# Seven products in place of eight: y times v_in by Strassen's scheme, with the combined weights kept in DRAM

## The chip, the cores and the metric

The kernel runs on one core of a Trainium2 chip. The metric is the device time of one execution in microseconds. All inputs lie in DRAM at the start, the output lies there at the end, and nothing is computed on the host except the layout of the inputs.

## The reference

Attention over 4 batches, 8 heads, 576 positions and 64 channels, with a causal window of 128 and a linear bias; then two gated layers over the 2304 tokens. Only the last lines matter for the change:

```python
attn_out = _attn_ref(q, k, v)                  # (4, 8, 576, 64)
x = attn_out.transpose(0, 2, 1, 3).reshape(2304, 512)
a = x @ w1; b = x @ w2                         # 512 -> 1024
y = ((a * b) @ w3) @ w_out                     # 1024 -> 1024 -> 512
h = y @ v_in                                   # 512 -> 2048   (moe2_w_in)
g = h * np.clip(h + 3.0, 0.0, 6.0) / 6.0
return (g @ v_out).astype(np.float32)          # 2048 -> 512   (moe2_w_out)
```

The weights arrive as 64-bit floats and are unpacked to 32-bit ones on the chip.

## The kernel before

Matrix products run in a 32-bit format that TensorE rounds. To keep the accuracy, each operand is split into a rounded part `hi` and the rest `lo` (`split`, L74: ACT copies, VectorE or GpSimd subtracts), and each product is three matmuls, hi x hi, hi x lo and lo x hi (`mm3`, L46 to L49). Each loads a 128x128 tile of one operand and streams the columns of the other.

The first half runs over batches: attention, then for each half batch of 288 tokens eight `ab_unit`s (a, b and their product) and four `y_unit`s (L504), which write y transposed to DRAM (`yT`). The matrices w3 and w_out are multiplied beforehand. During the last batch, at the units listed in `AT`, the weights of the second half are loaded (1 MB for each of 16 groups `f` of 128 of the 2048 columns of v_in, together with the matching rows of v_out), unpacked (`unpack`, L55) and split (`v2_split`, L523), and y of the first block is loaded and split too (`y_load`, `y_split`). The other groups follow during the second half's first block.

The second half runs over blocks of 512 tokens (four, and a last one of 256), and in each over the 16 groups. `h_unit` (L607) multiplies y by one group of v_in: four chunks of 128 channels, twelve matmuls into one bank, for which four banks of PSUM stand ready (two of `ps_mm`, two of `ps_h`). ACT applies the relu of h + 3 (L620), DVE takes the minimum with 6 times h (L621, the gate), and the result is split. `o_unit` (L627) multiplies it by v_out, 128 tokens at a time, into four banks that collect over all groups; it follows two units behind (`LAG`). All split weights stay in SBUF, 16 groups in hi and lo.

The order of the instructions on each engine is fixed when the program is built: the framework simulates a timeline and lists, for each engine, the ready instruction of the highest priority, so that the order can differ from that of the source. Instructions wrapped in `in_order(True, ...)` (L51) keep the order of the source among themselves. On the chip each engine then follows its list. Tiles with one tag share buffers, and a new tile waits until the old one is no longer read; a pool that is opened after others have been closed takes their room and waits for their last readers in the same way.

```python
units = [(j, f) for j in range(len(blocks)) for f in range(KG)]
LAG = 2
for idx, (j, f) in enumerate(units):
    h_unit(j, f)
    if idx >= LAG:
        o_unit(*units[idx - LAG])
```

Of the kernel before, what the change touches and what calls it, by code (L numbers as in the profile page):

```python
# [8 lines left out]
F32 = mybir.dt.float32  # L9
# [8 lines left out]
P = 128  # L18
# [4 lines left out]
def tile_attention_moe_moe2(ctx: ExitStack, tc: tile.TileContext, qT, kT, vm, vt, wo, w3, w12, w2x, out):  # L23
# [59 lines left out]
    yT = dpool.tile([KD, P, NT], F32, name="yT")  # L83
# [432 lines left out]
    TB = 512
    NPRE = 3
    v2 = {}

    def v2_load(f, tmp):  # L520
        load(("v2", f), w2x[f], tmp)

    def v2_split(f, pool, lo_eng):  # L523
        old = NPRE <= f < NPRE + KF
        hi, lo = (
            (blk if old else pool).tile(
                [P, 2 * KD, P], F32R, name=f"v2{t[0]}{f}", **({"tag": f"{t}{f - NPRE}"} if old else {})
            ) for t in ("hi", "lo")
        )
        split(flat(hi), flat(lo), unpack(rawt.pop(("v2", f)), pinned=True), lo_eng)  # L530
        v2[f] = (hi, lo)

    blocks = [(t, min(TB, NT - t)) for t in range(0, NT, TB)]
    yb = {}

    yraw = {}

    p2 = [("v", f) for f in range(KG)]
    p2.insert(NPRE, ("y", 0))

    def p2_load(i):
        if i < len(p2):
            (v2_load if p2[i][0] == "v" else y_load)(p2[i][1], dec)

    def p2_make(i, pool):
        if i < len(p2):
            if p2[i][0] == "v":
                v2_split(p2[i][1], pool, nc.vector)
            else:
                y_split(0, pool)  # L550
            p2_load(i + 2)

    def y_load(j, tmp):
        t0, n = blocks[j]
        t = tmp.tile([P, KD, TB], F32, tag="raw", name=f"yraw{j}")
        nc.sync.dma_start(out=t[:, :, 0:n], in_=yT[:, :, t0 : t0 + n].rearrange("c p t -> p c t"))
        yraw[j] = t

    def y_split(j, pool):
        t0, n = blocks[j]  # L560
        yh = pool.tile([P, KD, TB], F32R, tag="yh2", bufs=1, name=f"yh2_{j}")
        yl = pool.tile([P, KD, TB], F32R, tag="yl2", bufs=1, name=f"yl2_{j}")
        t = yraw.pop(j)
        for i in range(2):
            c = slice(2 * i, 2 * i + 2)
            nc.scalar.copy(yh[:, c, 0:n], t[:, c, 0:n])  # L566
            nc.gpsimd.tensor_tensor(out=yl[:, c, 0:n], in0=t[:, c, 0:n], in1=f32(yh[:, c, 0:n]), op=ALU.subtract)  # L567
        yb[j] = (yh, yl)
# [6 lines left out]
    for b in range(B):  # L575
        if b == B - 1:
            apool_ctx.close()
            ps_h = ctx.enter_context(tc.tile_pool(name="ps_h", bufs=2, space=PSUM))
            ps_o = ctx.enter_context(tc.tile_pool(name="ps_o", bufs=1, space=PSUM))

            AT = [3, 6, 9, 11, 13, 15, 17, 19, 21]
            dec = ctx.enter_context(tc.tile_pool(name="dec", bufs=2, side="right"))
            pre = ctx.enter_context(tc.tile_pool(name="pre", bufs=1, side="right"))
            p2_load(0)
            p2_load(1)
        for iu, u in enumerate(units):
# [12 lines left out]
    p1.close()  # L599


    vpool = ctx.enter_context(tc.tile_pool(name="vpool", bufs=1))
    r2 = ctx.enter_context(tc.tile_pool(name="r2", bufs=2))
    g2p = ctx.enter_context(tc.tile_pool(name="g2p", bufs=3))
    g2 = {}

    def h_unit(j, f):  # L607
        t0, n = blocks[j]
        yh, yl = yb[j]
        hi, lo = v2[f]  # L610
        if f % 2 == 0:
            ps = ps_mm.tile([P, 512], F32, tag="mm", name=f"h_{j}_{f}")
        else:
            ps = ps_h.tile([P, TB], F32, tag="h", name=f"h_{j}_{f}")
        for c in range(KD):
            mm3(ps[:, 0:n], hi[:, c, :], lo[:, c, :], yh[:, c, 0:n], yl[:, c, 0:n], c == 0, c == KD - 1)
        rl = r2.tile([P, TB], F32, tag="rl", name=f"rl_{j}_{f}")
        gh = g2p.tile([P, TB], F32R, tag="g2h", name=f"g2h_{j}_{f}")
        gl = g2p.tile([P, TB], F32R, tag="g2l", name=f"g2l_{j}_{f}")
        nc.scalar.activation(rl[:, 0:n], ps[:, 0:n], AF.Relu, bias=three[:, 0:1], scale=1.0)  # L620
        nc.vector.scalar_tensor_tensor(out=rl[:, 0:n], in0=rl[:, 0:n], scalar=6.0, in1=ps[:, 0:n], op0=ALU.min, op1=ALU.mult)  # L621
        split(gh[:, 0:n], gl[:, 0:n], rl[:, 0:n], nc.vector)
        g2[j, f] = (gh, gl)
# [21 lines left out]
    units = [(j, f) for j in range(len(blocks)) for f in range(KG)]
    LAG = 2
    for idx, (j, f) in enumerate(units):
        h_unit(j, f)
        if idx >= LAG:
            o_unit(*units[idx - LAG])  # L650
        if j == 0:
            p2_make(f + len(AT), vpool)
        if j + 1 < len(blocks):
            if f == KG - 3:
                y_load(j + 1, dec)
            if f == KG - 1:
                y_split(j + 1, pre if j % 2 else vpool)
    for u in units[-LAG:]:
        o_unit(*u)
# [61 lines left out]
```

## Time and profile before

| | |
|---|---|
| timed runs, median of 3 | 904.21 us (903.53 to 905.42) |
| profiled execution, span | 907.7 us, 3.5 us over that median |
| TensorE (PE) busy | 888.4 us, 98% |
| VectorE (DVE) busy | 435.3 us, 48% |
| ScalarE (ACT) busy | 402.0 us, 44% |
| GpSimd (POOL) busy | 143.4 us, 16% |
| DMA | 74.0 MB, mean 82 GB/s |
| mean granted clock of TensorE | 0.993 of 2.4 GHz |

The span is that of the profiled execution alone, from its first to its last instruction; all rows below are from it. Busy time of PE is time in which some matmul is under way; matmuls overlap, so a sum of durations says more than the time they cost, and the distance from the start of one to the start of the next is what one costs in a dense stream. PEld is the loading of the stationary operand, which runs beside the matmuls. In the rows, "a<-b" means that a is written from b; "[0.84 <-DVE rl L621]" behind an instruction is how long its engine stood idle before it, and what it waited for. SPq is the queue of the engine that issues most of the DMAs.

### The profile page before, as it was taken

The numbers are of one execution on the slowest core, as the hardware profiler recorded it, in microseconds if no ns is written. First come the engines' busy times: TensorE is split into PE (matmuls) and PEld (weight loads), VectorE is DVE, ScalarE is ACT, GpSimd is POOL, SyncE is SP. The second block draws the span as 40 slices with busy tenths as digits, with TensorE's granted clock in tenths as the row PEclk, the third lists the DMA queues.
The fourth block names the chain that finished last, engine by engine and source line by source line (L and its number), as shares of the span: only waits on it lengthen the run. The fifth ranks groups of instructions, "written<-read, shape, count | busy, mean of one in ns | idle before, by whom it ended". The sixth has DMA issues, their size and how long they took to land.

```text
span 907.7 us, 13401 instructions
## 1 busy us (share of the span) xinstructions
PE 888.4 (98%) x5216; PEld 780.2 (86%) x5216; DVE 435.3 (48%) x935; ACT 402.0 (44%) x856; POOL 143.4 (16%) x226
## 2 busy tenths in 40 slices
PE   6999899999999999999999999999999999999998
PEld 5645689999999999999999888888888888888897
DVE  6788565665766736451436587232223222322232
ACT  7566455665665645552334565322232222222232
POOL 5500302333331322220020002010010001000000
PEclk9999799999999999999999999999999999999999
DMA  9977312323332212103142455120001000100000
GB/s 272 287 294 262 92 60 66 93 66 85 72 79 60 63 52 66 40 2 119 47 166 93 165 186 189 43 70 1 1 1 46 1 1 1 47 1 1 17 30 24
DMA packets 23151, 74.00 MB, mean 82 GB/s; under 512 B 2864, under 2 KB 8496, under 8 KB 18480
## 3 DMA queue, kind: packets, MB, share of 16 engines
q1 hardware_dynamic: 23088, 73.15, 26.0%
q8 instruction: 41, 0.67, 0.3%
q14 instruction: 22, 0.18, 0.1%
HBM read 63.70 MB, written 9.44 MB: 81 GB/s over the span
## 4 chain that ended last, share of the span: by engine, by line
PE 88%; DMA 1%; ACT 0%; DVE 0%; POOL 0%; issue 0%; ACTq 0%
PE ab L47 8%; PE ab L48 8%; PE ab L49 8%; PE o L47 7%; PE o L49 7%; PE o L48 7%; PE h L47 7%; PE h L49 7%; PE h L48 7%; PE X L290 4%; PE y L47 4%; PE y L49 4%; PE y L48 3%; PE pt L261 2%; PE s L203 2%; PE s L206 1%
## 5 line engine op out<-in xcount | busy, mean ns | idle before, releaser
L47 PE MATMUL ab<-xh,w12h 128*128 128x288 f32 x512 | 155.6, 304 | 0.1
L48 PE MATMUL ab<-xl,w12h 128*128 128x288 f32 x512 | 152.0, 297 | 0.0
L49 PE MATMUL ab<-xh,w12l 128*128 128x288 f32 x512 | 151.6, 296 | 0.0
L621 DVE SCALAR_TENSOR_TENSOR rl<-rl,h 128x512 f32<-128x512 f32 (+1 forms) x80 | 50.7, 634 | 200.7 <-ACT rl L620 200.7
L620 ACT ACTIVATE rl<-h,three 128x512 f32<-128x512 f32 (+1 forms) x80 | 51.7, 647 | 200.5 <-PE h L49 196.5
L47 PE MATMUL h<-yh,v2h 128*128 128x512 f32 (+1 forms) x320 | 118.5, 370 | 0.8 <-DVE rl L621 0.8
L49 PE MATMUL h<-yh,v2l 128*128 128x512 f32 (+1 forms) x320 | 118.2, 369 | 0.0
L48 PE MATMUL h<-yl,v2h 128*128 128x512 f32 (+1 forms) x320 | 117.9, 368 | 0.0
L47 PE MATMUL o<-v2h,g2h 128*128 128x512 f32 x288 | 112.9, 392 | 0.0
L48 PE MATMUL o<-v2l,g2h 128*128 128x512 f32 x288 | 112.3, 390 | 0.0
L49 PE MATMUL o<-v2h,g2l 128*128 128x512 f32 x288 | 111.6, 391 | 0.0
L47 PEld LDWEIGHTS ab<-xh,w12h 128*128 128x128 f32 x512 | 96.5, 189 | 1.2 <-ACT asb L497 0.5
L48 PEld LDWEIGHTS ab<-xl,w12h 128*128 128x128 f32 x512 | 96.6, 189 | 0.5 <-issue 0.2
L49 PEld LDWEIGHTS ab<-xh,w12l 128*128 128x128 f32 x512 | 96.5, 188 | 0.0
L243 POOL TENSOR_SCALAR pr<-pr,rc 128x256 f32<-128x256 f32 (+1 forms) x128 | 61.4, 497 | 135.4 <-DVE rc L236 73.2
L76 DVE TENSOR_TENSOR g2l<-rl,g2h 128x512 fp32r<-128x512 f32 (+1 forms) x80 | 54.8, 685 | 44.6 <-ACT g2h L75 44.3
L47 PE MATMUL y<-g,Wh 128*128 128x288 f32 x256 | 75.9, 299 | 0.2 <-ACT yf L511 0.2
L567 POOL TENSOR_TENSOR yl<-yraw,yh 128x1024 fp32r<-128x1024 f32 (+1 forms) x10 | 24.0, 2423 | 327.2 <-ACT yh L566 327.2
L49 PE MATMUL y<-g,Wl 128*128 128x288 f32 x256 | 75.4, 297 | 0.0
L48 PE MATMUL y<-g,Wh 128*128 128x288 f32 x256 | 75.0, 295 | 0.0
L47 PEld LDWEIGHTS h<-yh,v2h 128*128 128x128 f32 x320 | 60.1, 188 | 12.1 <-DVE rl L621 1.3
L48 PEld LDWEIGHTS h<-yl,v2h 128*128 128x128 f32 x320 | 60.1, 188 | 11.0
(106 smaller groups left out, 1640.9 us busy)
## 6 DMA issues: line engine op xcount, KB each, us to landing
raww<-in_w_dram SPq DMA_DIRECT2D x16, 1024.0 KB, 6.6
rawv<-in_w2x_dram SPq DMA_DIRECT2D x16, 1024.0 KB, 4.9
rawq<-in_qT_dram SPq DMA_DIRECT2D x24, 288.0 KB, 4.3
rawk<-in_kT_dram SPq DMA_DIRECT2D x24, 288.0 KB, 4.6
yT<-yf SPq DMA_DIRECT2D x32, 144.0 KB, 1.8
out_dram<-ob SPq DMA_DIRECT2D x18, 256.0 KB, 2.0
rawwo<-in_wo_dram SPq DMA_DIRECT2D x4, 1024.0 KB, 8.3
yraw<-yT SPq DMA_DIRECT2D x4, 1024.0 KB, 5.2
```

Of the source, the lines that this page charges most:

```text
L47: nc.tensor.matmul(ps, lh, rh, start=first, stop=False)
L48: nc.tensor.matmul(ps, lh, rl, start=False, stop=False)
L49: nc.tensor.matmul(ps, ll, rh, start=False, stop=last)
L76: lo_eng.tensor_tensor(out=lo, in0=src, in1=f32(hi), op=ALU.subtract)
L203: in_order(n == NP + 1 and j == 0 and h == 0, nc.tensor.matmul(o, sp1["qs"][:, qc], sp1["kh"][:, kc], start=True, stop=False))
L206: nc.tensor.matmul(o, sp1["qs"][:, qc], sp1["kl"][:, kc], start=False, stop=True)
L243: nc.gpsimd.tensor_scalar(out=o, in0=o, scalar1=rc[:, 2 * j + h : 2 * j + h + 1], scalar2=1.0, op0=ALU.mult, op1=ALU.mult)
L261: nc.tensor.transpose(ps[:, o : o + P], prob[n, j][:, h, c : c + P], ident)
L290: last_pe["x", n, h] = nc.tensor.matmul(X[:, c0 : c0 + nq], l, r, start=bank not in seen, stop=last[bank] == idx, skip_group_check=True)
L567: nc.gpsimd.tensor_tensor(out=yl[:, c, 0:n], in0=t[:, c, 0:n], in1=f32(yh[:, c, 0:n]), op=ALU.subtract)
L620: nc.scalar.activation(rl[:, 0:n], ps[:, 0:n], AF.Relu, bias=three[:, 0:1], scale=1.0)
L621: nc.vector.scalar_tensor_tensor(out=rl[:, 0:n], in0=rl[:, 0:n], scalar=6.0, in1=ps[:, 0:n], op0=ALU.min, op1=ALU.mult)
```

## The change

The 2304 tokens are taken in three blocks of 768, each as two halves of 384 tokens; the 512 channels are two halves, and the 16 groups of v_in are paired, group p with group p + 8. For each block and pair, y times v_in is then a product of 2x2 blocks, made with seven products (the Winograd form of Strassen's scheme) in place of eight: sums of y's quarters (`y_sums`, GpSimd) and of v_in's quarters (`va_make`, GpSimd) are made first, and seven products (`PRODUCTS`) of two chunks each, 384 columns wide, go through the two banks of `ps_mm`. DVE adds them up to the four results (`s1`, `u2`, `u3`, c22, c21, c12); one result is added up in PSUM alone. `ps_h` is gone; the products with v_out collect in six banks. They are cut into twelve `o_jobs` per pair, which are put between the products of the next pair (`QUOTA`).

The combined weights of a pair, seven tiles in hi and lo, are 14 KB per partition, so not all fit in SBUF: each is stored in DRAM (`vad`, and `vod` for v_out) once made, and fetched again in each later block (`fetch`, two pairs ahead). Four of the eight pairs are made in the last batch of the first half, the other four in block 0, at its even positions. The pools of the second half (`ypool` first) are opened when all of the first half's are closed; `blk`, which outlived the first half before, is now among those. y of block 0 is therefore loaded after the first half's last use of that room, by ACT's queue; the loads of later blocks stand in SP's queue, in the order of the source, with the fetches and stores. The split tiles of y have one buffer each.

```diff
-    yT = dpool.tile([KD, P, NT], F32, name="yT")
+    yT = dpool.tile([2, KD // 2, P, NT], F32, name="yT")
+    NPR = KG // 2
+    vad = dpool.tile([NPR, P, 2, 7, 2 * P], F32, name="vad")
+    vod = dpool.tile([NPR, P, 2, 2, DM], F32, name="vod")
...
-    blk = ctx.enter_context(tc.tile_pool(name="blk", bufs=1))
     p1 = ExitStack()
+    blk = p1.enter_context(tc.tile_pool(name="blk", bufs=1))
...
+    PRODUCTS = [(A11, B11), (S2, T2), (A12, B21), (S3, T3), (S1, T1), (A22, T4), (S4, B22)]
+    def dma(dst, src):
+        in_order(not p1_open[0], nc.sync.dma_start(out=dst, in_=src))
...
+    def va_tile(p, right):
+        pool = vR if right else vL
+        va[p] = pool.tile([P, 2, 7, 2 * P], F32R, tag="va", bufs=2, name=f"va{p}")
+    def vo_tile(p, right):
+        vo[p] = pool.tile([P, 2, 2, DM], F32R, tag="vo", bufs=1 if right else 2, name=f"vo{p}")
+    def va_make(p, right):
+        r = unpack(rawt.pop(("v2", 2 * p)), pinned=True)
+        q = [r[:, i * 2 * P : (i + 1) * 2 * P] for i in range(4)]
+        st = sR.tile([P, 3, 2 * P], F32, tag="st", name=f"st{p}")
+        nc.gpsimd.tensor_tensor(out=st[:, 0, :], in0=q[0], in1=q[2], op=ALU.subtract)
+        nc.gpsimd.tensor_tensor(out=q[2], in0=q[2], in1=q[3], op=ALU.add)
+        nc.gpsimd.tensor_tensor(out=st[:, 1, :], in0=q[2], in1=q[0], op=ALU.subtract)
+        nc.gpsimd.tensor_tensor(out=st[:, 2, :], in0=q[1], in1=st[:, 1, :], op=ALU.subtract)
+        t = va_tile(p, right)
+        split(flat(t[:, 0, 0:4, :]), flat(t[:, 1, 0:4, :]), r, nc.vector)
+        split(flat(t[:, 0, 4:7, :]), flat(t[:, 1, 4:7, :]), flat(st), nc.vector)
+        late.append((vad[p], t))
...
+    def y_load(j):
+        for ci in range(2):
+            t = ypool.tile([P, 2, 2 * TH], F32, tag=f"yraw{ci}", name=f"yraw{j}_{ci}")
+            src = yT[ci, :, :, 2 * TH * j : 2 * TH * (j + 1)].rearrange("c p t -> p c t")
+            if j == 0:
+                nc.scalar.dma_start(out=t, in_=src)
             else:
+                dma(t, src)
+            yraw[j, ci] = t
+    def y_sums(j):
+        for ci in range(2):
+            t = yraw.pop((j, ci)).rearrange("p c (h t) -> p (c h) t", h=2)
+            tm = ypool.tile([P, 3, TH], F32, tag=f"tm{ci}", name=f"tm{j}_{ci}")
+            nc.gpsimd.tensor_tensor(out=tm[:, 0, :], in0=t[:, 3, :], in1=t[:, 1, :], op=ALU.subtract)
+            nc.gpsimd.tensor_tensor(out=t[:, 1, :], in0=t[:, 1, :], in1=t[:, 0, :], op=ALU.subtract)
+            nc.gpsimd.tensor_tensor(out=tm[:, 1, :], in0=t[:, 3, :], in1=t[:, 1, :], op=ALU.subtract)
+            nc.gpsimd.tensor_tensor(out=tm[:, 2, :], in0=tm[:, 1, :], in1=t[:, 2, :], op=ALU.subtract)
...
+    def y_splits(j):
+        for _, k in PRODUCTS:
+            hi = ypool.tile([P, 2, TH], F32R, tag=f"yh{k}", name=f"yh{j}_{k}")
+            lo = ypool.tile([P, 2, TH], F32R, tag=f"yl{k}", name=f"yl{j}_{k}")
+            for ci in range(2):
+                split(hi[:, ci, :], lo[:, ci, :], yraw.pop((j, ci, k)), nc.vector)
...
-            ps_h = ctx.enter_context(tc.tile_pool(name="ps_h", bufs=2, space=PSUM))
-            AT = [3, 6, 9, 11, 13, 15, 17, 19, 21]
+            AT = [2, 5, 8, 10, 12, 14, 16, 18]
...
+    def h_pair(j, p, between):
+        a, b_ = bank(0), None
+        product(0, a, True, True)
+        s1 = new("s1")
+        nc.scalar.copy(s1, a[:, 0:TH])
+        between(0)
+        b_ = bank(1)
+        product(1, b_, True, True)
+        u2 = new("u2")
+        nc.vector.tensor_tensor(out=u2, in0=b_[:, 0:TH], in1=s1, op=ALU.add)
+        between(1)
+        product(2, a, False, True)
+        gate(a[:, 0:TH], (0, 0))
+        between(2)
+        product(3, b_, False, True)
+        u3 = new("u3")
+        nc.vector.tensor_tensor(out=u3, in0=b_[:, 0:TH], in1=s1, op=ALU.add)
+        between(3)
+        a = bank(2)
+        product(4, a, True, True)
+        c = new("c22")
+        nc.vector.tensor_tensor(out=c, in0=a[:, 0:TH], in1=u3, op=ALU.add)
+        gate(c, (1, 1))
+        between(4)
+        b_ = bank(3)
+        product(5, b_, True, True)
+        c = new("c21")
+        nc.vector.tensor_tensor(out=c, in0=u3, in1=b_[:, 0:TH], op=ALU.subtract)
+        gate(c, (1, 0))
+        between(5)
+        product(6, a, False, True)
+        c = new("c12")
+        nc.vector.tensor_tensor(out=c, in0=a[:, 0:TH], in1=u2, op=ALU.add)
+        gate(c, (0, 1))
+        between(6)
...
+    QUOTA = [2, 2, 2, 1, 2, 2, 1]
+    y_load(0)
+    y_sums(0)
+    y_splits(0)
...
+    for n, (j, pos) in enumerate(units):
+        p = ORDER[j][pos]
+        if n == 0:
+            fetch(1)
+        fetch(n + 2)
...
+        gs = h_pair(j, p, between)
+        jobs = o_jobs(j, pos, gs, vo[p])
+        if j + 1 < NBLK:
+            if pos == NPR - 4:
+                y_load(j + 1)
+            if pos == NPR - 2:
+                y_sums(j + 1)
+            if pos == NPR - 1:
+                y_splits(j + 1)
```

`product(i, ps, first, last)` is six matmuls (`mm3` for two chunks); `gate` is relu, gate and split of one result, as in `h_unit`; `bank(n)` takes the next tile of `ps_mm`.

## Rows read from the trace of the kernel before

**Rows 1.** The page: busy time, share of the span and instructions of each engine.

```profile
span 907.7 us, 13401 instructions
...
PE 888.4 (98%) x5216; PEld 780.2 (86%) x5216; DVE 435.3 (48%) x935; ACT 402.0 (44%) x856; POOL 143.4 (16%) x226
```

**Rows 2.** Two stretches of the second half: length, busy time by engine, clock, DMA.

```profile
515.00:560.00 45.00, 44.16 (x193) 35.81 (x192) 36.34 (x44) 29.99 (x37) 0.00 (x0) 1.00 0.47 167
...
600.00:850.00 250.00, 250.00 (x1095) 205.25 (x1094) 67.53 (x97) 64.84 (x100) 8.24 (x4) 1.00 0.04 13
```

**Rows 3.** Groups by form: line, engine, tiles, count | busy, mean ns | idle before.

```profile
L620 ACT ACTIVATE rl<-h,three 128x512 f32<-128x512 f32 x64 | 44.1, 690 | 176.9 <-PE h L49 173.0 <-DMA yT<-yf 4.0
L621 DVE SCALAR_TENSOR_TENSOR rl<-rl,h 128x512 f32<-128x512 f32 x64 | 43.9, 688 | 176.8 <-ACT rl L620 176.8
L75 ACT CAST g2h<-rl 128x512 fp32r<-128x512 f32 x64 | 39.8, 622 | 40.7 <-DVE rl L621 40.6
...
L500 DVE TENSOR_TENSOR asb<-ab,asb 128x288 f32<-128x288 f32 x64 | 29.2, 456 | 62.4 <-PE ab L49 52.5 <-PE pt L261 9.2 <-ACT xf L303 0.3
...
L76 POOL TENSOR_TENSOR xl<-xf,xh 128x288 fp32r<-128x288 f32 x30 | 25.1, 853 | 49.7 <-ACT xh L75 49.7
...
L567 POOL TENSOR_TENSOR yl<-yraw,yh 128x1024 fp32r<-128x1024 f32 x8 | 21.0, 2650 | 244.6 <-ACT yh L566 244.6
...
L76 DVE TENSOR_TENSOR v2l<-rawv,v2h 128x1024 fp32r<-128x1024 f32 x16 | 20.0, 1250 | 11.6 <-ACT v2h L75 11.6
L69 DVE SCALAR_TENSOR_TENSOR rawv<-rawv 128x1024 int32<-128x1024 int32 x16 | 19.6, 1226 | 7.1 <-ACT rawv L64 6.4
...
L65 DVE TENSOR_SCALAR rawv<-rawv 128x1024 int32<-128x1024 int32 x16 | 11.0, 690 | 2.0 <-DMA rawv<-in_w2x_dram 2.0
...
L620 ACT ACTIVATE rl<-h,three 128x256 f32<-128x256 f32 x16 | 7.6, 476 | 23.6 <-PE h L49 23.5
...
L621 DVE SCALAR_TENSOR_TENSOR rl<-rl,h 128x256 f32<-128x256 f32 x16 | 6.7, 421 | 23.9 <-ACT rl L620 23.9
L75 ACT CAST g2h<-rl 128x256 fp32r<-128x256 f32 x16 | 6.5, 406 | 7.5 <-DVE rl L621 7.5
```

**Rows 4.** Timeline of one unit of 512 tokens: start, length, engine, operation.

```profile
641.73 0.39 PE L49 MATMUL h<-yh,v2l 128*128 128x512 f32 x1
...
642.21 0.69 ACT L620 ACTIVATE rl<-h,three 128x512 f32<-128x512 f32 x1 [3.38 <-PE h L49]
...
642.93 0.69 DVE L621 SCALAR_TENSOR_TENSOR rl<-rl,h 128x512 f32<-128x512 f32 x1 [3.37 <-ACT rl L620]
```

**Rows 5.** A stretch of the last y units alone (288 columns).

```profile
499.00:511.00 12.00, 12.00 (x93) 12.00 (x92) 1.20 (x3) 1.00 0.64 212
```

**Rows 6.** Timeline, last block: relu of its fourth and its fifteenth unit.

```profile
866.00 0.47 ACT L620 ACTIVATE rl<-h,three 128x256 f32<-128x256 f32 x1 [1.26 <-PE h L49]
...
896.68 0.48 ACT L620 ACTIVATE rl<-h,three 128x256 f32<-128x256 f32 x1 [1.43 <-PE h L49]
```

**Rows 7.** Instructions of h alone, during the last batch of the first half.

```profile
460.00:490.00 30.00, 6.53 (x24) 4.23 (x24) 0.00 (x0) 0.00 (x0) 1.00 0.41 144
```

**Rows 8.** Timeline where the second half starts.

```profile
516.34 1.26 ACT L620 ACTIVATE rl<-h,three 128x512 f32<-128x512 f32 x2 [3.95 <-DMA yT<-yf]
...
517.80 0.50 PE L47 MATMUL h<-yh,v2h 128*128 128x512 f32 x1 [0.84 <-DVE rl L621]
```

**Rows 9.** DMA: the weights' loads on the page; the first 50 us.

```profile
rawv<-in_w2x_dram SPq DMA_DIRECT2D x16, 1024.0 KB, 4.9
...
DMA packets 2998, 14.45 MB, mean 289 GB/s; under 512 B 431, under 2 KB 623, under 8 KB 1775
```

**Rows 10.** Timeline in block 0, POOL and DVE.

```profile
560.91 4.81 POOL L567 TENSOR_TENSOR yl<-yraw,yh 128x1024 fp32r<-128x1024 f32 x2 [91.77 <-ACT yh L566]
...
563.77 2.49 DVE L76 TENSOR_TENSOR g2l<-rl,g2h 128x512 fp32r<-128x512 f32 x1 [0.69 <-ACT g2h L75]
```

**Rows 11.** A stretch of the first half with gaps of PE.

```profile
100.00:150.00 50.00, 47.75 (x288) 40.36 (x288) 32.59 (x72) 27.72 (x61) 11.15 (x20) 0.93 0.20 57
```

More of the change, by code (lines that the diff above doesn't have):

```diff
@@ L559, in y_split @@
[L559 to L568, printed above, removed]
+        nc.sync.dma_start(out=yT[d % 2, d // 2, :, t0 : t0 + HS], in_=yf)
@@ L599, in tile_attention_moe_moe2 @@
     p1.close()
-    vpool = ctx.enter_context(tc.tile_pool(name="vpool", bufs=1))
+    p1_open[0] = False
+    ypool = ctx.enter_context(tc.tile_pool(name="ypool", bufs=1))
+    vL = ctx.enter_context(tc.tile_pool(name="vL", bufs=1))
     r2 = ctx.enter_context(tc.tile_pool(name="r2", bufs=2))
[L604 to L623, printed above, removed]
@@ L645, in tile_attention_moe_moe2 @@
[L645 to L659, printed above, removed]
+    g2p = ctx.enter_context(tc.tile_pool(name="g2p", bufs=8))
@@ new lines, in tile_attention_moe_moe2, with product, new, gate @@
+    po = {}
+    ob_ = {}
+    def h_pair(j, p, between):
+        w = va[p]
+        def product(i, ps, first, last):
+            k, y = PRODUCTS[i]
+            yh, yl = yc[j, y]
+            for c in range(2):
+                cols = slice(c * P, (c + 1) * P)
+                mm3(
+                    ps[:, 0:TH], w[:, 0, k, cols], w[:, 1, k, cols], yh[:, c, :], yl[:, c, :],
+                    first and c == 0, last and c == 1, skip_group_check=True,
+                )
+        def new(tag):
+            return r2.tile([P, TH], F32, tag=tag, bufs=2 if tag in ("rl", "u2", "u3") else 1, name=f"{tag}_{j}_{p}")
+        gs = {}
+        def gate(h, q):
+            rl = new("rl")
+            g_ = g2p.tile([P, 2, TH], F32R, tag="g2", name=f"g2_{j}_{p}_{q[0]}{q[1]}")
+            nc.scalar.activation(rl, h, AF.Relu, bias=three[:, 0:1], scale=1.0)
+            nc.vector.scalar_tensor_tensor(out=rl, in0=rl, scalar=6.0, in1=h, op0=ALU.min, op1=ALU.mult)
+            split(g_[:, 0, :], g_[:, 1, :], rl, nc.vector)
+            gs[q] = g_
+        def bank(n):
+            return ps_mm.tile([P, 512], F32, tag="mm", name=f"h_{j}_{p}_{n}")
+        a, b_ = bank(0), None
[32 more added lines that the diff above has]
+        between(6)
+        return gs
@@ new lines, in tile_attention_moe_moe2, with fetch @@
+    QUOTA = [2, 2, 2, 1, 2, 2, 1]
+    units = [(j, pos) for j in range(NBLK) for pos in range(NPR)]
+    def fetch(n):
+        if n >= len(units):
+            return
+        j, pos = units[n]
+        p = ORDER[j][pos]
+        if j == 0 and p >= NEARLY:
+            return
+        if not (j == 0 and p >= NEARLY - 2):
+            dma(f32(va_tile(p, pos % 2 == 0)), vad[p])
+        if not (j == 0 and p == NEARLY - 1):
+            dma(f32(vo_tile(p, pos % 2 == 0)), vod[p])
+    y_load(0)
+    y_sums(0)
@@ L662 @@
+    for job in jobs:
+        job()
 _OUTS = [((2304, 512), "float32")]
```

164 lines of the change are left out of this document (102 added, 62 removed).

## The prediction

> **What bounds the kernel now.** Read the busy times first: PE 888.4 us of a 907.7 us span, DVE and ACT under half [rows 1]. The stretches then show that this holds in the second half, which the change rewrites: from 600 to 850 us PE is busy for 250.00 of 250.00 us with 1095 matmuls, DVE for 67.5 us; only from 515 to 560, while weights are still being made, do DVE (36.3 of 45) and ACT come near it [rows 2]. The by-form rows price the DVE, ACT and POOL instructions [rows 3]. The timeline of one unit shows what follows an h matmul group: relu, then gate, then cast and subtract, the gate 0.03 us after the relu's end [rows 4]. So a matmul taken away is worth its spacing, and a new wait of PE costs its whole length.
>
> **The matmuls.** Spacing, not duration, is what one costs, for they overlap. 512 columns: 250.00/1095 = 0.2283 us [rows 2]. 288 columns: 12.00/93 = 0.129, say 0.130 since a matmul on an edge is counted [rows 5]. 256 columns: eleven units of the last block take 896.68 - 866.00 = 30.68 us, 2.789 each; less six out-matmuls (1.370) leaves 1.419 for twelve: 0.118 [rows 6]. There is no 384 in the trace. Between 256 and 512 it is 0.173, between 288 and 512 it is 0.172; I take 0.173. Its bounds are the pro rata values, 0.171 from 512 and 0.1775 from 256.
>
> Before, h has 64 units of 12 at 512 columns and 16 of 12 at 256: 768 x 0.2283 + 192 x 0.118 = 198.0 us. After, 3 blocks x 8 pairs x 7 products x 6 = 1008 at 0.173: 174.4 us. **Saved: 23.6 us** (19 to 25.5 by the bounds). The products with v_out are 864 of 512 columns before and after, 197 us: no change. A pair is now 42 x 0.173 + 36 x 0.2283 = 15.5 us of PE. The matmuls of h that now run early, 24 between 460 and 490 us [rows 7], are only moved, and cost nothing if the first half had no gaps that they filled; if it had, they hid up to 6.5 us. I take 1 us, since matmuls of ab and y fill the other time there.
>
> **DVE and ACT per pair.** For 384 columns halfway between the rows of 256 and 512: relu 0.583, gate 0.555, cast 0.514; the adds and the subtract I take at 0.555 too (the 288-column multiply took 0.456) [rows 3]. A pair is 5 adds, 4 gates, 4 subtracts: 13 x 0.555 = 7.2 us of DVE in 15.5; ACT's copy, 4 relus and 4 casts are under 5. Neither bounds a pair alone.
>
> **The edge of a pair.** h loses the two banks of `ps_h`: its seven products now go through two. The last one (product 6) ends in a bank that the next pair's product 0 wants. Between them stands one out-job. The add of c12 can start 0.48 us after the last matmul's start in [rows 4], at 384 columns some 0.42; with 0.555 and 0.03 it frees the bank at 1.01 us. PE has that matmul (0.173) and three of 512: 0.86 us. So it falls short by 0.15 us, 24 times: **3.6 us**. Below: nothing, if more out-jobs are put in between when the program is ordered. Above: if DVE takes gate (1,0)'s subtract first, that chain (add, relu, gate, cast, subtract and four hops) ends 3.30 us after product 5's last matmul, against 2.83 when c12 could start: 0.47 more, 0.62 per pair, 15 us.
> The trace has one wait of this kind: at 517.80, with all four banks of h full, PE waited 0.84 us until the gate had freed one [rows 8]. The Trainium skill (Perfetto Trace Analysis, Matmuls) says that independent groups should rotate through different PSUM banks, so that one is emptied while the next is computed; the change goes from four to two. If the rule is taken to mean that each pair pays such a wait, the term is 24 x 0.84 = 20 us in place of 3.6; the wait agrees with it in kind, and nothing here shows it for each pair.
>
> **Where the second half starts.** Before, y of block 0 was loaded and split during the first half. Now its room is free only after the last ab unit; four y units (96 matmuls, 12.5 us) cover. The first product needs one part of the two loads (5 us by the 1024 KB loads of [rows 9]), two casts, two subtracts: about 7 us, covered. The second needs T2, the third of four sums per half, and POOL computes them: 0.853 us at 288 columns, 2.65 at 1024, so 1.09 at 384 [rows 3]; seven of them after the load make 13 us and the split 14, against 13.5 when it is due. Then pair 0 has no out-jobs between its products, 7.3 us of PE, while DVE has 14 subtracts (7.8 us), the pair's 7.2 and v_in's combinations for pair 1: shift 0.69, unpack 1.23, subtract 1.25 and 0.94 for the extra three quarters, 4.1 us. I take **5 us**. Below: 0. Above: 19, the second rival.
> One thing there is worse than the sum of busy times: at 563.77 a subtract of 512 columns took 2.49 us in place of 0.69, while POOL was at work from 560.91 to 565.72 [rows 10]. If sums and subtracts take turns like this, the seventh sum ends 7 x 1.09 + 6 x 0.555 = 11 us after the load, T2 is split at 17 and product 1 is some 3.5 us late; my 5 us contain that. The Trainium skill (SBUF — State Buffer, Who interferes with whom) says that a DVE instruction with two SBUF inputs and a GpSimd instruction that reads SBUF contend for one port pair. By it they do take turns; without it product 1 would be 0.5 us late, and the term about 2.
>
> **Two changes of block.** y's split tiles are single now, so block j+1's splits wait for pair 7's products: 14 subtracts more in 31 us of two pairs, 22 us of DVE. That fits; the list of instructions is ordered ahead of time, and in [rows 7] it moved h forward by 40 us, so I expect them spread. 1 us each: **2 us**, from 0 to 12 (all splits behind the last product).
>
> **Block 0 makes weights.** Four pairs x 7.3 us of DVE (4.1, and 3.17 for v_out), pairs 8 x 7.2, splits 7.8: 95 of 124 us, 76%; before, 81% left PE at 44.2 of 45 [rows 2]. With two banks in place of four, a 1.2 us unpack in front of an eviction shows: **2 us**, 0 to 10.
>
> **The stream.** Each pair of blocks 1 and 2 fetches 1.84 + 1.05 = 2.89 MB in 15.5 us: 186 GB/s. The first 50 us ran at 289 GB/s [rows 9]. SP issues in order, and the fetch of a right-hand v_out tile waits for the out-jobs of the pair before it, so two pairs' transfers bunch: the next v_in tile lands some 2.89/0.289 = 10 us plus a couple after, inside 15.5. Also y (1.57 MB) fits once: 15.4, tight. Block 0 moves 11.5 MB of stores, 8.4 of raw weights and 6.8 fetched again: 215 GB/s, under 289 too. I take 0.
>
> **Sum.** 907.7 - 23.6 + 1 + 3.6 + 5 + 2 + 2 = 897.7 us in the profiled execution's terms. Its span lies 3.5 us over the timed median of 904.2, so the forecast is **894 us**.
>
> **Rivals.**
> *All covered* (0.17): the order fills every edge, start and block change cost under 5 us together: 880 to 888. For it: PE idled 0.84 us in the second half of before although DVE was at 81%. Against it: four banks then, and a second half already prepared.
> *The two-bank ring* (0.15): 0.62 us per pair in place of 0.15, 15 us: 905.6, about even; alone it would eat the saving from 0.98 us per pair. For it: c12 has no cover beyond one job, and DVE is a queue in order. Against it: the order can be chosen so that c12 goes first.
> *The start drains PE* (0.15), the one that ends slower. Place: y's loads of block 0 stand in ACT's queue behind the four copies of y. If they stay behind the last, the load starts as PE runs dry: 8 us for two loads, 1.1 of splits, 3 for T2, 4 in DVE-bound pair 0 and some 3 of a lower clock (granted, on the mean of its levels of 1.2 and 2.4 GHz, 0.93 from 100 to 150 us, where PE had gaps [rows 11]): 19 us in place of 5: 908. Beyond about 14 us of idle PE there the saving is gone. For it: before, ACT at 516.34 stood 3.95 us behind a store of y [rows 8]. Against it: nothing orders the loads behind the copies but the list's order.
> *The stream is late* (0.08): if transfers and bunching deliver 167 GB/s (the mean of 515 to 560 [rows 2], though there not asked for more), a pair takes 17.3 us, 1.8 more, 16 times: 922. It decides from 186 GB/s down.
>
> **How the numbers follow.** Forecast 894 with 0.45; its own range, edges and start between half and twice their price, 889 to 901. The range 882 to 916 leaves out the best of the first rival and the worst of the last two. A measurement here tells 0.2%, 1.8 us, from no change: faster is forecast and first rival, 0.62; the ring falls half within 0.2% (0.08) and half slower; with the start and the stream, slower is 0.30.
>
> **What would show it.** Right: 1008 matmuls of 128x384 some 0.173 us apart; PE idle at the start under 6 us, waiting for DVE or POOL; under 0.3 us at a pair's edge, releaser the add of c12. Wrong: spacing near 0.178; waits of the first product of every pair over 0.6 us; PE waiting for DMA of va in blocks 1 and 2; a granted clock under 1 after the start.

## The result and the profile after

| | before | after |
|---|---|---|
| median | 904.21 us (903.53 to 905.61, 5 runs) | 910.49 us (909.56 to 914.2, 5 runs) |
| profiled execution, span | 907.7 us | 907.5 us |

The ratio is 1.0067, 95% interval 1.0044 to 1.0089: the change makes the kernel 6.3 us slower; forecast was a kernel 10 us faster. The two profiled executions have nearly the same span only because that of before was among its longest: in 18 later runs of before the time went from 902.07 to 909.94 us, and a run's time is its span plus about 2.1 us. So a second profile of before was taken, and it serves as the measure below (span 902.5).

The page of after, as [rows 1]:

```profile
span 907.5 us, 13963 instructions
...
PE 875.2 (96%) x5264; PEld 787.6 (87%) x5264; DVE 540.5 (60%) x1137; ACT 434.0 (48%) x952; POOL 180.2 (20%) x272
```

Less work for PE, and 2% more of the span without it. The stretches of after, to be read beside [rows 2] (columns as there: length, busy time and count of PE, PEld, DVE, ACT, POOL, then clock, DMA share, GB/s):

```profile
460.00:500.00 40.00, 36.50 (x263) 34.90 (x262) 26.11 (x34) 20.78 (x33) 9.18 (x11) 1.00 0.81 297
500.00:515.00 15.00, 11.13 (x65) 9.99 (x65) 13.60 (x17) 8.63 (x22) 8.87 (x7) 0.89 0.58 190
515.00:545.00 30.00, 29.67 (x145) 26.03 (x144) 20.16 (x33) 13.01 (x21) 3.33 (x4) 1.00 0.60 225
545.00:590.00 45.00, 43.56 (x212) 37.58 (x210) 31.41 (x46) 21.43 (x33) 9.04 (x8) 1.00 0.65 261
590.00:620.00 30.00, 29.21 (x144) 25.82 (x145) 17.90 (x30) 11.50 (x20) 1.56 (x2) 1.00 0.70 267
620.00:650.00 30.00, 25.43 (x112) 20.70 (x111) 29.16 (x40) 17.37 (x34) 15.24 (x11) 0.94 0.57 214
650.00:850.00 200.00, 199.99 (x988) 178.14 (x988) 98.13 (x184) 69.12 (x133) 8.68 (x8) 1.00 0.54 216
```

From 650 on PE is dense: 988 matmuls in 200 us are 15.79 us for a pair's 78, at 216 GB/s of stream. Every loss lies where POOL is at work: the last batch of the first half (460 to 500), the start (500 to 515), the four makes of block 0, and worst 620 to 650, where POOL works 15 of 30 us and DVE is busy for 29. The second profile of before, in the first of these stretches:

```profile
460.00:500.00 40.00, 40.00 (x285) 38.95 (x284) 20.91 (x30) 16.70 (x28) 4.49 (x2) 1.00 0.39 139
```

What PE waits for in after, from 500 to 660 us (line waited for: total, times, longest):

```profile
PE h L48 <- DVE yl L76: 3.6, 2, 3.0
PE o L49 <- DVE g L76: 2.9, 4, 1.8
PE h L47 <- DVE rl L679: 1.6, 2, 1.3
PE h L47 <- ACT va L75: 1.5, 1, 1.5
```

DVE's results, or ACT's that come just before. And what DVE does there, in two stretches of its timeline (start, length, operation; "x3" is three instructions in a row, given as one line from the start of the first to the end of the last):

```profile
501.74 3.96 DVE L76 TENSOR_TENSOR yl<-yraw,yh 128x384 fp32r<-128x384 f32 x3
...
510.38 1.48 DVE L76 TENSOR_TENSOR yl<-tm,yh 128x384 fp32r<-128x384 f32 x3
...
618.19 0.55 DVE L712 TENSOR_TENSOR c<-u,h 128x384 f32<-128x384 f32 x1
...
620.68 1.37 DVE L76 TENSOR_TENSOR g<-rl,g 128x384 fp32r<-128x384 f32 x1
621.98 1.35 DVE L65 TENSOR_SCALAR rawv<-rawv 128x1024 int32<-128x1024 int32 x1
623.25 0.55 DVE L717 TENSOR_TENSOR c<-h,u 128x384 f32<-128x384 f32 x1
...
625.21 1.35 DVE L76 TENSOR_TENSOR g<-rl,g 128x384 fp32r<-128x384 f32 x1
```

while POOL runs

```profile
503.95 1.33 POOL L600 TENSOR_TENSOR tm<-tm,yraw 128x384 f32<-128x384 f32 x1
...
507.92 1.19 POOL L600 TENSOR_TENSOR tm<-tm,yraw 128x384 f32<-128x384 f32 x1
...
620.30 1.34 POOL L597 TENSOR_TENSOR tm<-yraw 128x384 f32<-128x384 f32 x1
621.60 1.18 POOL L560 TENSOR_TENSOR st<-rawv 128x256 f32<-128x256 f32 x1
622.74 1.47 POOL L598 TENSOR_TENSOR yraw<-yraw 128x384 f32<-128x384 f32 x1
```

Three subtracts take 3.96 us beside POOL's sums and 1.48 after the last of them (it ends at 509.11): 1.32 each against 0.49. It is [rows 10] over and over. The instructions that read PSUM (c<-u,h, c<-h,u) keep their 0.55 us in the midst of it. Where DVE has slack, the same costs PE nothing: POOL's sums for block 2 are the 8.68 us of POOL in the stretch 650 to 850, in which PE is busy for 199.99 us of 200.

One more row, the waits of SP's queue in block 0 (500 to 660 us; total, times, longest): the fetch of a right-hand v_out tile has a single buffer and stands in front of the raw weights, and SP issues nothing for up to 32 us until the out-jobs have freed it.

```profile
SPq L538 <- PE o L49: 98.0, 4, 32.4
```

**The theory**: sums on POOL and DVE's work take turns, everywhere and not only at the start, and this is what the gain was spent on; the queue behind SP adds to it by letting the makes of the last pair of block 0 fall together with the sums of y for block 1. **The rivals**: DVE is simply full while weights are made; the time is in the start and in the spacing of the matmuls; what costs is the chain of sums, slow on POOL, and not the turns.

### The profile page after: what moved, and what is told of

The parts are those of the page before. It is cut to its first block, busy times and chain, and to the rows that moved or that the text cites. A ratio compares the mean times of both kernels' runs of the same rounds, so it can differ in the third digit from the quotient of the medians.

```text
span 907.5 us, 13963 instructions
## 1 busy us (share of the span) xinstructions
PE 875.2 (96%) x5264; PEld 787.6 (87%) x5264; DVE 540.5 (60%) x1137; ACT 434.0 (48%) x952; POOL 180.2 (20%) x272
## 4 chain that ended last, share of the span: by engine, by line
PE 79%; DVE 6%; DMA 2%; ACT 2%; issue 1%; POOL 0%; DVEq 0%; SPq 0%; ACTq 0%
PE ab L47 7%; PE ab L48 7%; PE ab L49 7%; PE o L47 7%; PE o L48 7%; PE o L49 6%; PE h L47 6%; PE h L49 6%; PE h L48 6%; PE X L293 4%; PE y L49 4%; PE y L47 4%; PE y L48 3%; PE pt L264 2%; DMA rawv<-in_w2x_dram 2%; DVE yl L76 2%
## 5 line engine op out<-in xcount | busy, mean ns | idle before, releaser
L47 PE MATMUL h<-yh,va 128*128 128x384 f32 x336 | 116.0, 345 | 3.3 <-DVE rl L679 1.6
L48 PE MATMUL h<-yl,va 128*128 128x384 f32 x336 | 114.0, 339 | 3.6 <-DVE yl L76 3.6
L49 PE MATMUL h<-yh,va 128*128 128x384 f32 x336 | 114.0, 340 | 0.8 <-DVE va L76 0.7
L47 PE MATMUL o<-vo,g 128*128 128x512 f32 x288 | 113.7, 395 | 0.4 <-ACT g L75 0.3
L48 PE MATMUL o<-vo,g 128*128 128x512 f32 x288 | 113.4, 394 | 0.0
L49 PE MATMUL o<-vo,g 128*128 128x512 f32 x288 | 86.6, 394 | 3.0 <-DVE g L76 2.9
L678 ACT ACTIVATE rl<-c,three 128x384 f32<-128x384 f32 x72 | 44.3, 617 | 82.0 <-DVE c L706 44.0
L47 PEld LDWEIGHTS h<-yh,va 128*128 128x128 f32 x336 | 63.7, 190 | 13.4 <-DVE rl L679 6.1
L48 PEld LDWEIGHTS h<-yl,va 128*128 128x128 f32 x336 | 63.8, 190 | 7.8 <-DVE yl L76 4.2
L76 DVE TENSOR_TENSOR g<-rl,g 128x384 fp32r<-128x384 f32 x96 | 56.4, 590 | 20.4 <-ACT g L75 17.4
L49 PEld LDWEIGHTS o<-vo,g 128*128 128x128 f32 x288 | 53.6, 188 | 14.9 <-DVE g L76 4.8
L230 ACT ACTIVATE pr<-pr,mn 128x256 f32<-128x256 f32 (+1 forms) x128 | 60.4, 474 | 12.1 <-DVE mn L221 12.0
```

Source lines behind the costliest of these rows:

```text
L47: nc.tensor.matmul(ps, lh, rh, start=first, stop=False, **kw)
L48: nc.tensor.matmul(ps, lh, rl, start=False, stop=False, **kw)
L49: nc.tensor.matmul(ps, ll, rh, start=False, stop=last, **kw)
L76: lo_eng.tensor_tensor(out=lo, in0=src, in1=f32(hi), op=ALU.subtract)
L230: nc.scalar.activation(o, o, AF.Exp, bias=mn[:, col : col + 1], scale=-1.0, accum_out=sm[:, col : col + 1])
L678: nc.scalar.activation(rl, h, AF.Relu, bias=three[:, 0:1], scale=1.0)
```

## The experiments

Times are medians; ratios are to runs of before on the same chip (904.5 to 905.0 us). "Second half" is the distance, in each profile, from the start of the last y matmul to that of the last out-matmul but one; "middle" that from the start of the first ab matmul to that of the last y matmul. These leave out the first 115 us or so, whose length differs by 5.2 us between the two profiles of before, all of the difference of their spans. At most some 3.4 us of it are the clock (0.03 x 115, an estimate): the granted clock of these 115 us has a mean of 0.96 of its higher level (2.4 GHz) in the first profile and of 0.99 in the second.

| kernel | us | ratio, 95% interval | middle | second half |
|---|---|---|---|---|
| before, second profile | 904.67 (one) | | 392.6 | 391.2 |
| after, run again | 910.05 | 1.0072 (1.0049 to 1.0096) | 390.9 | 399.6 |
| no makes in block 0 | 895.99 | 0.9920 (0.9884 to 0.9955) | 390.6 | 386.9 |
| all sums on DVE | 895.39 | 0.9906 (0.9875 to 0.9937) | 388.6 | 386.6 |
| late fetch of v_out | 903.89 | 0.9994 (0.9973 to 1.0015) | 391.2 | 392.9 |
| sums on DVE, late fetch | 892.85 | 0.9874 (0.9845 to 0.9904) | 388.2 | 386.0 |
| v_in's sums on DVE | 906.41 | 1.0017 (0.9993 to 1.0042) | 389.1 | 396.0 |
| y's sums on DVE | 903.50 | 0.9985 (0.9967 to 1.0003) | 390.6 | 393.3 |
| sums on DVE, idle work on POOL | 924.39 | 1.0216 (1.0186 to 1.0246) | 393.7 | 410.4 |
| sums on DVE, no makes | 890.40 | 0.9858 (0.9839 to 0.9877) | 387.1 | 382.6 |
| sums on DVE, late fetch, y earlier | 896.43 | 0.9909 (0.9885 to 0.9932) | 389.9 | 386.1 |

In the first profile of after the two stretches were 391.2 and 396.6.

**Before, again.** No edit.

> The kernel before, unchanged, for a second profile. Both theories expect a time within 0.3% of 904.2 us; it tells how the profiled execution's own time stands to the median (in the first profile of before it lay about 5 us above) and whether the spacing of the 512-column matmuls, 0.2266 us in two stretches of 55 us of the second half and 0.2305 elsewhere, falls in the same places again.

904.67 us, span 902.5. First half and second half are as long as in the first profile (392.6 against 392.1, 391.2 against 391.7); the 5.2 us between the spans lie ahead of the first ab matmul. That y ended at 505.6 us in after and at 511.2 in the first profile of before was therefore chance, not a gain.

**After, again.** No edit.

> The changed kernel, unchanged, on the chip of the experiments. Both theories: 909 to 912 us, with the stalls of 3.5 us at 460 to 500 and of 6 us at the start in the same places; if these places lose much less in this profile, what was read from the first profile was chance.

910.05 us; the stalls are there again (PE 37.14 of 40 us at 460 to 500, 15.66 of 20 at 500 to 520).

**No makes in block 0.** Block 0 makes no weights, and the stored ones of pairs 0 to 3 stand in for those of pairs 4 to 7, so half of the pairs use wrong weights.

```diff
-            dma(f32(va_tile(p, pos % 2 == 0)), vad[p])
+            dma(f32(va_tile(p, pos % 2 == 0)), vad[p % NEARLY])
...
-                if k == 2:
-                    va_make(q, False)
...
-                if k == 4:
-                    vo_make(q, False)
...
```

> Leaves out that block 0 makes the combined weights of pairs 4 to 7: the stored ones of pairs 0 to 3 are fetched in their place in all blocks, so the output uses wrong weights for half of the pairs. Theory 'block 0': the loss of the second half is made by these weights being made while block 0 runs, late behind SP's queue and with GpSimd and VectorE in each other's way; the profile of after shows PE short of its pace by 1.8 us at 543 to 561, 2.2 at 575 to 593 and 7.9 at 618 to 645, 11.9 together; they go, the start (some 6 us) stays: 898 to 900 us. Rival 'start and pace': the forecast was missed by the start and by matmuls that are spaced wider than I took, and the makes are covered: 907 to 910.

895.99 us, 14 less than after. The makes of block 0, with the loads and stores that belong to them, cost 14 us where I had taken 2. Two of its stretches (columns as above, here and below):

```profile
545.00:590.00 45.00, 45.00 (x226) 40.41 (x225) 21.11 (x39) 14.44 (x27) 0.00 (x0) 1.00 0.32 129
...
620.00:650.00 30.00, 29.99 (x150) 26.55 (x149) 20.26 (x42) 15.79 (x33) 0.00 (x0) 1.00 0.47 193
```

PE has no gap, although the splits of y for block 1 are still there. This says where the time is, not yet why: the makes are DVE's work, POOL's and SP's at once.

**All sums on DVE.** All eight lines of sums, four for v_in and four for y, go from `nc.gpsimd` to `nc.vector`.

```diff
-        nc.gpsimd.tensor_tensor(out=st[:, 0, :], in0=q[0], in1=q[2], op=ALU.subtract)
+        nc.vector.tensor_tensor(out=st[:, 0, :], in0=q[0], in1=q[2], op=ALU.subtract)
...
-            nc.gpsimd.tensor_tensor(out=tm[:, 0, :], in0=t[:, 3, :], in1=t[:, 1, :], op=ALU.subtract)
+            nc.vector.tensor_tensor(out=tm[:, 0, :], in0=t[:, 3, :], in1=t[:, 1, :], op=ALU.subtract)
```

> Moves the sums of y and of v_in's combinations of block 0 and of the first half's last pairs from GpSimd to VectorE; computes the same. Theory 'the two engines take turns': a VectorE subtract of 384 columns took 1.3 to 1.4 us beside GpSimd sums where 0.555 is its price alone, so with no GpSimd sums the start loses 4 us in place of 6 and 618 to 645 loses 4 in place of 7.9: 903 to 906. Rival 'VectorE is full': its 13 to 16 added sums per pair at about 0.5 us come on top of a queue that was busy 20.00 of 20 us at 620 to 640: 912 to 916.

895.39 us: 15 less than after, twice or more of what the theory expected, and the contrary of "VectorE is full".

```profile
460.00:500.00 40.00, 39.09 (x292) 38.62 (x291) 31.99 (x52) 25.02 (x44) 0.00 (x0) 1.00 0.83 305
500.00:515.00 15.00, 12.79 (x68) 10.94 (x66) 14.14 (x28) 8.00 (x14) 0.00 (x0) 1.00 0.84 292
...
620.00:650.00 30.00, 28.54 (x141) 24.87 (x140) 23.49 (x47) 14.99 (x30) 0.00 (x0) 1.00 0.75 289
```

With more instructions on DVE it is busy for less: 47 in 23.49 us at 620 to 650 against 40 in 29.16. The gain came in all three places, in the first half too, which I had not counted. Part of it is the clock: here it is 1.00 in all three, where after had 0.89 and 0.94 in two of them, worth at most some 3.4 us (0.11 x 15 + 0.06 x 30, an estimate), and the second profile of after has more of this (0.83 at 500 to 520).

**Late fetch of v_out.** `fetch_right(n)` is called at the start of the pair that uses the tile, before `fetch(n + 2)`.

```diff
-        if not (j == 0 and p == NEARLY - 1):
-            dma(f32(vo_tile(p, pos % 2 == 0)), vod[p])
+        if pos % 2:
+            dma(f32(vo_tile(p, False)), vod[p])
+    def fetch_right(n):
+        j, pos = units[n]
+        p = ORDER[j][pos]
+        if pos % 2 == 0 and not (j == 0 and p == NEARLY - 1):
+            dma(f32(vo_tile(p, True)), vod[p])
...
+        fetch_right(n)
```

> The fetch of a right-hand v_out tile, which waits for the out-jobs that still read its only buffer, is issued at the start of its own pair and not two pairs ahead; computes the same. Theory 'SP is blocked': in block 0 SP issued nothing for up to 32 us at a time behind this fetch, so the raw weights of the next pair came late and their making fell together with the sums of y for block 1; issued freely, the making spreads and the loss of 11.9 us at 543 to 645 falls to 4 or 5: 902 to 904. Rival 'VectorE and GpSimd are simply full in block 0': no change, 909 to 911. Second rival: the tile now lands too late for its out-jobs, PE waits for DMA in blocks 1 and 2, and the time is over 912.

903.89 us: 6 to 7 less than after, as the theory had it. But SP did not become free; it now stands as long before the stores of what is being made (500 to 660 us):

```profile
SPq L538 <- DVE va L76: 98.4, 7, 29.2
```

What changed is the meeting at the end of block 0. The sums of y for block 1 now run from 608.55 to 617.17 and v_in's from 619.39 on, one after the other, where after had both from 618.36 to 635.32:

```profile
590.00:620.00 30.00, 29.97 (x141) 26.45 (x142) 16.30 (x27) 9.31 (x18) 8.90 (x9) 0.94 0.80 316
620.00:650.00 30.00, 28.75 (x138) 24.34 (x137) 26.47 (x45) 20.29 (x38) 3.29 (x4) 1.00 0.70 278
```

Losses elsewhere stayed (545 to 590: PE 42.83 of 45 us). So the head of the queue mattered by what it pushed together, which is less than my theory said.

**Both.** The two edits together.

> Both: all sums on VectorE, and the fetch of a right-hand v_out tile issued at the start of its own pair; computes the same. Theory 'two causes': the sums on VectorE alone gave 895.4 us and the free SP queue alone took 6.6 us off the kernel after; with the sums on VectorE the pairs of block 0 still lose 6 us between 545 and 635, and earlier raw weights halve that: 891 to 893. Rival 'one cause': the late weights cost time only because GpSimd and VectorE then got in each other's way; with no sums on GpSimd nothing is left to win: 895 to 896.

892.85 us, 1.3% under before and the fastest version that computes the same. Against sums on DVE alone the intervals overlap and the second halves are 386.0 and 386.6 us: that the late fetch is worth something without POOL beside it isn't shown. Two of its stretches, with what is left to lose:

```profile
500.00:515.00 15.00, 12.73 (x64) 10.62 (x63) 14.14 (x28) 8.69 (x15) 0.00 (x0) 1.00 0.87 307
...
620.00:650.00 30.00, 29.79 (x147) 26.04 (x146) 21.00 (x42) 15.48 (x33) 0.00 (x0) 1.00 1.00 396
```

**One kind of sum alone.** First those of v_in (as above, the first pair of lines only), then those of y (the second pair only).

> Only the sums of v_in's combinations on VectorE, those of y stay on GpSimd; computes the same. Theory 'turns': PE was short by 3.5 us between 460 and 500 us in the kernel after, where GpSimd makes sums of v_in, and by 4 us at 543 to 593; these go, as does half of 618 to 645, and the start with y's sums stays: 900 to 903 us. Rival 'y alone': all that the move of the sums gained came from the sums of y at the start and at 618 to 645: 908 to 910.

> Only the sums of y on VectorE, those of v_in stay on GpSimd; computes the same. Theory 'turns': the start loses some 3 us less and 618 to 645 some 4 us less than in the kernel after, the stalls at 460 to 500 and at 543 to 593 stay: 902 to 904 us; with the run before it, the two gains add up to the 15 us of both. Rival 'v_in alone': no change, 909 to 911.

906.41 and 903.50 us. By the ratios 5.0 and 7.9 us of 15.0: each move helps, and together they give 2 us more than their sum, which the intervals can't tell from none. The stretch 460 to 500, where nearly only v_in's sums fall, shows the first alone (PE 38.51 of 40), the stretch 500 to 515 the second (12.37 of 15). With v_in's sums on DVE and y's on POOL:

```profile
460.00:500.00 40.00, 38.51 (x287) 38.04 (x286) 30.55 (x45) 23.25 (x40) 3.61 (x3) 1.00 0.85 305
500.00:515.00 15.00, 11.22 (x59) 10.18 (x58) 13.07 (x19) 6.87 (x14) 6.42 (x6) 0.89 0.71 238
```

and the other way round:

```profile
460.00:500.00 40.00, 37.35 (x273) 36.12 (x272) 28.26 (x38) 21.56 (x36) 7.15 (x8) 1.00 0.82 302
500.00:515.00 15.00, 12.37 (x69) 10.33 (x68) 13.56 (x27) 9.20 (x18) 2.64 (x4) 1.00 0.70 233
```

**Idle work on POOL.** The sums on DVE, and beside them as many subtracts on POOL whose result nobody reads:

```diff
+        dum = dp.tile([P, TH], F32, tag="dum", name=f"dv{p}")
+        for _ in range(4):
+            nc.gpsimd.tensor_tensor(out=dum[:, 0 : 2 * P], in0=q[0], in1=q[1], op=ALU.subtract)
...
+            dum = dp.tile([P, TH], F32, tag="dum", name=f"dy{j}_{ci}")
+            for _ in range(4):
+                nc.gpsimd.tensor_tensor(out=dum, in0=t[:, 3, :], in1=t[:, 2, :], op=ALU.subtract)
```

> All sums on VectorE as in the run that gave 895.4 us, and beside them GpSimd does as many subtracts of the same sizes on the same tiles, whose result nobody reads; computes the same. Theory 'turns': what costs is that GpSimd works beside VectorE, so VectorE's subtracts are stretched again and most of the 15 us comes back: 905 to 912. Rival 'chain': what cost was that a GpSimd sum takes 1.0 to 1.3 us where VectorE takes 0.55 and the next step waits for it; subtracts that nobody waits for cost nothing: 895 to 897.

924.39 us: work that no sum waits for costs 29 us. This is what tells turns from the chain. Two stretches of it, to be read beside those of all sums on DVE:

```profile
500.00:515.00 15.00, 10.37 (x57) 9.04 (x55) 15.00 (x21) 6.79 (x16) 8.42 (x7) 0.77 0.30 100
...
620.00:650.00 30.00, 23.11 (x95) 19.25 (x94) 29.31 (x39) 13.81 (x24) 14.71 (x12) 0.83 0.39 148
```

DVE is busy almost without a break, and PE's gaps are followed by stretches of a lower clock. DVE's timeline in two places,

```profile
499.01 1.38 DVE L600 TENSOR_TENSOR tm<-yraw 128x384 f32<-128x384 f32 x1
500.31 1.37 DVE L76 TENSOR_TENSOR yl<-yraw,yh 128x384 fp32r<-128x384 f32 x1
...
624.86 1.09 DVE L558 TENSOR_TENSOR st<-rawv 128x256 f32<-128x256 f32 x1
625.87 0.54 DVE L719 TENSOR_TENSOR c<-u,h 128x384 f32<-128x384 f32 x1
```

and POOL's in the first of them:

```profile
498.19 5.64 POOL L606 TENSOR_TENSOR dy<-yraw 128x384 f32<-128x384 f32 x4 [7.30 <-DMA yraw<-yT]
```

The very sums that take 0.55 us (384 columns) and 0.42 (256) with POOL at rest take 1.38 and 1.09, and POOL's take 1.41 each; the add that has one operand in PSUM takes 0.54. The idle subtracts also hold the raw tiles longer, so part of the 29 us may be later loads; the durations don't depend on that. Up to some 9 of the 29 are the lower clock of these two stretches (0.23 x 15 + 0.17 x 30, an estimate). It may be worse than after because the sums themselves are now among the stretched work of DVE; that was not tested apart. The Trainium skill (SBUF — State Buffer, Who interferes with whom) says that a DVE instruction with two SBUF inputs contends with a GpSimd instruction that reads SBUF, since its second input comes through an interface that the two engines share; these durations agree. It also says that a `tensor_scalar` can enter a mode that contends in the same way; the one-input shift L65, a `tensor_scalar` of 0.69 us in [rows 3] and 1.35 in after, agrees.

**No makes, sums on DVE.** The first two edits together.

> All sums on VectorE, and block 0 makes no weights (it fetches the stored ones of pairs 0 to 3 in the place of 4 to 7, so half of the pairs use wrong weights). It prices the makes of block 0 when nothing works beside VectorE: with them and the sums on VectorE the time was 895.4 us, and PE lost 6 us between 545 and 635. Theory 'makes cost even then': 889 to 891. Rival 'without GpSimd they are covered, and what is lost at 605 to 635 is block 1's sums and splits of y': 893 to 895.

890.40 us, as the theory had it: with the sums on DVE the makes cost 4 to 5 us, with those on POOL 14. In its stretches of block 0 PE has no gap:

```profile
545.00:590.00 45.00, 45.00 (x224) 40.13 (x223) 19.72 (x37) 13.50 (x26) 0.00 (x0) 1.00 0.34 133
590.00:620.00 30.00, 30.00 (x148) 26.63 (x148) 18.83 (x37) 11.81 (x25) 0.00 (x0) 1.00 0.60 243
```

**y earlier.** Both edits, and the next block's y a pair earlier.

```diff
-            if pos == NPR - 4:
+            if pos == NPR - 5:
                 y_load(j + 1)
-            if pos == NPR - 2:
+            if pos == NPR - 3:
                 y_sums(j + 1)
```

> All sums on VectorE, the late fetch of right-hand v_out tiles, and the load and the sums of y for the next block one pair earlier, in the stretch of a pair that makes no weights; computes the same. Theory 'VectorE is full only where they meet': PE lost 2.9 us at 605 to 635 in the version without this, of which 2 go: 890 to 891.5. Rival: they meet the makes one pair earlier or keep the buffers longer, and nothing changes: 892 to 894.

896.43 us, a miss. The second half is as long as without it (386.1 against 386.0): 605 to 635 lost 1.3 us less and 575 to 605 lost 1.8 more, so the meeting only moved. The rest of the difference lies ahead of the second half, where PE's instructions stand in the same order; the intervals of this run and of "sums on DVE, late fetch" overlap.

## Why the prediction was wrong, point by point

By starts of matmuls; what a stretch lost is its time beyond the normal spacing of its matmuls (0.175 us at 384 columns, 0.2305 at 512):

| term | forecast | measured in after |
|---|---|---|
| matmuls of h, and the spacing of those with v_out | -23.6 | -21 |
| first half without its h matmuls | +1 | +4 |
| pair edges | +3.6 | next to nothing at the edges; +2 inside the pairs of blocks 1 and 2 |
| start | +5 | +7 |
| block 0's makes and the change to block 1 | +3 | +12 |
| change to block 2, stream | +1 | under 0.5 |
| sum | -10 | +4 |

The +4 is that of the two stretches of this profile (391.2 + 396.6 us against 392.6 + 391.2); in the second profile of after it is 6.7, and the medians differ by 6.3. Block 0's own waits of the kind in the row "pair edges" are in the two rows below it.

**The matmuls** were sized well: 0.175 us apart at 384 columns for 0.173. Those with v_out came 0.2305 apart for 0.2283: 1008 x 0.175 + 864 x 0.2305 = 375.6 us, against 391.2 of before and 5.5 of its 24 early ones (24 x 0.2283).

**The pair edge** was right in size alone, by luck. A pair takes 15.79 us against 42 x 0.175 + 36 x 0.2305 = 15.65, so 0.14 over, near the 0.15 forecast. But it is not lost at the edge, and the add of c12 (L717), the releaser that I named, stands behind a single wait of 0.3 us in 15 pairs. PE waits in the middle of every second pair: product 4 wants the bank of product 2, which the gate of the first result (L679) still reads, and there only one out-matmul stands between products 3 and 4 (waits of the weight loads from 660 to 900 us: total, times, longest; then one of them).

```profile
PEld h L47 <- DVE rl L679: 2.8, 8, 0.4
PEld h L47 <- DVE c L717: 0.3, 1, 0.3
...
701.02 0.55 DVE L679 SCALAR_TENSOR_TENSOR rl<-rl,h 128x384 f32<-128x384 f32 x1 [4.93 <-ACT rl L678]
...
701.24 0.39 PE L49 MATMUL o<-vo,g 128*128 128x512 f32 x1
...
701.62 0.19 PEld L47 LDWEIGHTS h<-yh,va 128*128 128x128 f32 x1 [0.36 <-DVE rl L679]
```

With the weight load that then stands bare, it is 0.26 us each time. The ring of two banks does cost something, then, but not where the forecast or its rival had it; 0.62 a pair, and the 0.84 of a rule taken to the letter, are excluded. DVE's price, 0.555 us at 384 columns, is right where POOL rests, as the groups by form of 650 to 850 us show (columns as in [rows 3]):

```profile
L76 DVE TENSOR_TENSOR g<-rl,g 128x384 fp32r<-128x384 f32 x50 | 27.9, 560 | 13.4 <-ACT g L75 11.6
...
L701 DVE TENSOR_TENSOR u<-h,s 128x384 f32<-128x384 f32 x13 | 7.2, 556 | 5.0 <-PE h L49 5.0
```

**The start** lost 6.0 us to 515 and 1.0 to 527, for 5, and not by the rival: the loads of y were issued at 493.19, ahead of the last copies. Nor was it quite where the forecast had it: the longest wait is in the first product, which I had called covered, for the lo part of its second chunk.

```profile
509.58 0.44 PE L48 MATMUL h<-yl,va 128*128 128x384 f32 x1 [2.95 <-DVE yl L76]
```

The turns of sums and subtracts that I named there are about half of it: with all sums on DVE the same stretch loses 3.7 us, where I had put "about 2" without turns. POOL's eight sums took 1.28 us in the mean (1.00 to 1.88) for the 1.09 taken. After PE's gaps the granted clock fell too, to a mean of 0.89 of its higher level (2.4 GHz) at 500 to 515, some 1.6 of the 6.0 us; the sum had a lower clock only in a rival.

**The step that failed is "Block 0 makes weights"**, 2 us from 0 to 10. The row has +12, with 1 taken for the change to block 1. The step added up DVE's instructions at the prices they have alone, 95 of 124 us, and left out that each make brings four sums on POOL. The turns that I had read from [rows 10] and priced at the start hold here as well: beside POOL a subtract costs 1.37 us for 0.555. From 620 to 650 DVE is then busy for 29.16 of 30 us, PE for 25.43. Taking the sums off POOL gave back 15 us, adding idle ones took 29. The 2 us were too few even without turns: with the sums on DVE the makes still cost 4 to 5. In the same way the first half's term missed the three makes with sums between 457 and 494: 4 us for 1, of which 2.6 came back with the sums on DVE. And the queues, which I read for the stream alone ("I take 0", right for blocks 1 and 2: dense PE at 216 GB/s), had a head in block 0 that let makes and sums of y meet: 6 to 7 us while the sums are on POOL.

What made it slower is thus none of the rivals that I let end slower, but another cause: a helper engine that slows the engine it helps. With the sums on DVE and the late fetch the kernel takes 892.85 us, near the 894 forecast; that isn't the sum confirmed, since its terms are others (the start 3.7, block 0 still some 5).

## What to carry to other kernels

Before work is moved to GpSimd, look up in the trace what VectorE does in those microseconds: where its instructions read two operands from SBUF, each can be held up for most of one of GpSimd's (0.55 us became 1.37 here; a GpSimd sum of that size took 1.00 at the least), and 0.55 us of VectorE may replace 1.3 us of both. It costs time where VectorE has no slack, as in block 0, and none where it has, as between blocks 1 and 2. A price that depends on a neighbour must be charged at every place where the neighbour works, not at the one where it was noticed. And compare a change with two profiles of before, cut at the same instructions: a start that differs by 5 us from run to run had hidden the whole result.

## What the runs showed of the hardware

In both profiles of before the 512-column matmuls of the second half come 0.2267 us apart in two stretches of 50 us (620 to 670 and 795 to 845) and some 0.230 on average between them, at a granted clock of 1.00 in either; in after they come 0.2305 apart from 650 to 850. DMA is not what differs: from 720 to 760 it moves nothing in the first profile, and the spacing is 0.2305. It is worth 1 to 2 us, it repeats, and its cause stays open. Nothing was run on it.
